# Three chained networks on one core: local attention heads in units of 32 queries and 64 keys, and one block's strided products queued in an earlier group

## The chip, the cores and the metric

The kernel runs on one core of a Trainium2 chip. The metric is the device time of one execution in microseconds, so less is better. Engines are named as in the profile: PE is TensorE (PEld its weight loads), DVE is VectorE, ACT is ScalarE, POOL is GpSimd, and SP is the queue that issues most of the transfers.

## What is computed

An attention over 4 sequences of 576 tokens with 8 heads of 64 is followed by two networks over the 2304 tokens, each fed with the output of the one before. Cut to what matters:

```python
scores = scale * np.matmul(q, k.transpose(0, 1, 3, 2))
rel = pos[:, None] - pos[None, :]
mask_local = (rel >= 0) & (rel < 32)                      # heads 0 to 3
mask_strided = (rel >= 0) & (pos[None, :] % 32 == pos[:, None] % 32)   # heads 4 to 7
attn = softmax(np.where(mask, scores, -1e9))
x = (attn @ v) as 2304 x 512
h = x @ w_in;  x = (h - np.tanh(h)) @ w_out               # d_ff 2048
xn = x / rms(x) * rms_g
x = (silu(xn @ w_gate) * (xn @ w_val)) @ w_out2           # d_ff 1536
```

A query of a local head sees itself and the 31 tokens ahead of it. A query of a strided head sees the tokens of its own residue modulo 32.

## The kernel before, in words

**Blocks and groups.** The tokens are cut into 9 blocks of 256 (block 4 is made of the last 64 tokens of each of the four sequences). The first network runs over five groups of blocks, (0,1), (2,3), (4), (5,6) and (7,8), with 16 steps in each. In a step TensorE makes a tile of h (`ps_h`, 12 matrix products), ACT its tanh, DVE the difference (`tg`, function `dve_g`), ACT and DVE split that in two parts (`g`), and TensorE adds the tile of an earlier step to the output (`ps_x`, 12 products). After the last group the second network follows; it has no attention work in it.

**Attention beside it.** While group g runs, the attention of the blocks of group g+1 is made. Class `Local` has the local heads of a block, and runs in stages: `st_s` (scores, TensorE), `st_m` and `st_e` (mask, maximum, exponential, for each of two halves of 128 queries), `st_n` (normalisation on DVE), `st_p` (transposes on TensorE, into `ps_p`) with `st_c` (copy into `pT`), `st_v` (product with the values, TensorE, into `ps_v`) and `st_o` (copy and split into `xs`, the input of the network). In words of the hand-written opening these are the letters s, m, e, n, p, c, v, y and z. Before the change a unit is 64 queries against 96 keys. The strided heads are either `Dense` (the same stages, with a mask, blocks 0 to 3 and 6) or `Strided` (blocks 4, 5, 7 and 8): there GpSimd multiplies queries by keys (`qk_item`, tile `pr`) and DVE reduces that into `sc`; after a softmax (`soft`, tile `se`) GpSimd multiplies the values by the weights (`pv_item`, tile `pr`), DVE reduces that into `so`, transposes it and splits it into `xs` (`fin`). There are three buffers for `pr`, and one each for the strided queries `sq`, keys `sk` and values `sv`, which `Dense` uses too: a load of them waits until the block before is through with its own.

**What sets the order.** The opening, `START`, is written by hand for all engines. Group 0 is ordered by the compiler's scheduler. From group 1 to group 3 TensorE's order is that of the program; DVE, ACT and GpSimd are ordered by the scheduler, and the SP queue by the scheduler until the last group (in group 0 by hand). `Work` holds two lists for the blocks to come: `.pe`, stages that run at the steps in `STINT`, and `.st`, the strided products, spread over the steps by their size. `EARLY = (5,)` names the block whose strided queries and keys are multiplied in group 1, right behind those of block 4. The products of queries and keys of block 7 stand in the list of group 3 (the fourth), in which the attention of blocks 7 and 8 is made.

```python
SOON = {2: 6, 3: 2}
STINT = {1: (4, 6, 8, 11, 14), 2: (1, 3, 6, 7, 9, 10, 13), 3: (1, 4, 6, 8, 11, 13)}
```

A step runs in this order: h, tanh, the stages of `.pe`, `dve_g`, the items of `.st`, the two parts of g, and then the output product of an earlier step.

Of the kernel before, what the change touches and what calls it, by code (L numbers as in the profile page):

```python
# [33 lines left out]
def attn_moe_moe_kernel(  # L34
# [3 lines left out]
    near_v: bass.AP,  # L38
# [4 lines left out]
    v_loc: bass.AP,  # L43
# [20 lines left out]
    W = 32  # L64
# [34 lines left out]
    EARLY = (5,)  # L99
# [18 lines left out]
    tab = one.tile([128, 544], F32, name="tab")  # L118
    ident, mask, dmask = tab[:, 192:320], tab[:, 320:416], tab[:, 416:544]
    add = tab[:, 0:192].bitcast(BF16)  # L120
    ident16, add = add[:, 0:128], {96: add[:, 128:320].rearrange("q (u t) -> q u t", u=2), 64: add[:, 320:384]}
# [228 lines left out]
    class Heads:  # L350
        def __init__(self, j):
            self.j, self.near, self.early = j, j < NEAR, j < EA
            self.ps, self.sm, self.nm, self.ss, self.pp, self.pT, self.v = {}, {}, {}, {}, {}, {}, {}
            self.slot, self.both, self.sums = {}, None, None
            self.fused = False
# [9 lines left out]
        size = {"sm": 512, "pT": 512, "v": 512}  # L365

        def st_s(self, bank):
# [3 lines left out]
            for hh in range(2):  # L371
                if self.early:
                    m = add[w]
                    m = m.unsqueeze(2) if w == 96 else m.unsqueeze(1).unsqueeze(1)
# [12 lines left out]
        def st_m(self, i):  # L387
# [10 lines left out]
            self.ss[i] = att.tile([128, 2, 2], F32, tag="ss", name="ss", bufs=4)  # L398
            m = dmask if w == 128 else mask if not self.near else add[96][:, i] if w == 96 else add[64]
# [22 lines left out]
        def st_n(self, i):  # L422
            sm, ss = self.sm[i], self.ss.pop(i)
# [3 lines left out]
                out=sm, in0=sm, in1=ss.unsqueeze(3).to_broadcast([128, 2, 2, self.w]), op=ALU.mult  # L427
# [27 lines left out]
    class Local(Heads):  # L455
        w = 96

        def __init__(self, j):
            super().__init__(j)
            self.runs = runs(j)  # L460
            self.at, self.kw = [], 0
            if self.near:
                self.at, self.kw = [0, 32, 96, 160], SUB
            else:
                for _, _, n, _ in self.runs:
                    self.at += range(self.kw, self.kw + n, 64)
                    self.kw += W + n

        def load_qk(self):
# [6 lines left out]
            for b, t0, n, x0 in self.runs:  # L476
# [4 lines left out]
                o = self.at[x0 // 64]  # L481
                nc.sync.dma_start(out=self.kT[:, :, o:o + W + n], in_=k_loc[b, :, :, t0 - W:t0 + n])

        def load_v(self, i):
            if self.early:
                t = held.tile([128, 1024], F32, tag="v", name="v")[0:96]
                nc.sync.dma_start(out=t, in_=near_v[self.j])
                for i in range(2):
                    self.v[i] = t[:, 512 * i:512 * i + 512].rearrange("k (u f) -> k u f", u=2)
                return  # L490
            t = self.room("v", i, 512)[0:96]
            self.v[i] = t.rearrange("k (u f) -> k u f", u=2)
            if self.near:
                nc.sync.dma_start(out=t, in_=near_v[self.j, :, 512 * i:512 * i + 512])
                return
# [943 lines left out]
```

## Time and profile before

| what | value |
|---|---|
| median of 3 runs | 889.43 us (888.55 to 890.35) |
| the profiled execution, its own time | 887.7 us |
| its span | 885.9 us |
| granted clock of TensorE | 0.996 |
| PE busy | 868.8 us (98%) |
| DVE busy | 668.5 us (75%) |
| ACT busy | 397.9 us (45%) |
| POOL busy | 280.0 us (32%) |

The span begins with the first instruction and ends with the last; 1.8 us of the profiled execution's own time lie outside it. The profiled execution is 1.7 us below the median. Times in the rows of the trace count from the start of the span.

### The profile page before, as it was taken

How to read it: one execution, taken by the hardware profiler on the slowest of the kernel's cores; microseconds unless marked ns; L12 is line 12 of the kernel's file. 1: busy time of each engine (PE TensorE's matmuls, PEld its weight loads, DVE VectorE, ACT ScalarE, POOL GpSimd, SP SyncE). 2: the span in 40 equal slices, each digit the busy share in tenths (PEclk: the TensorE clock that was granted, in tenths of full speed). 3: DMA queues.
4: the chain of work that ended last, by engine and by line, in shares of the span. 5: the costliest groups of instructions: out<-in, count | busy, mean ns of one | idle time of the engine just before them, and what ended most of it. 6: DMA issues, size and time to landing. Idle time of an engine off the chain costs nothing.

```text
span 885.9 us, 14105 instructions
## 1 busy us (share of the span) xinstructions
PE 868.8 (98%) x5091; PEld 739.7 (83%) x5091; DVE 668.5 (75%) x1376; ACT 397.9 (45%) x897; POOL 280.0 (32%) x315
## 2 busy tenths in 40 slices
PE   6999999999999999999999999999999999999998
PEld 4888888888998887888887888888878988888986
DVE  5999788888779887179978898576997953445444
ACT  6987643332544333265637553355332533422320
POOL 0000147695276952000000569676442400000000
PEclk8999999999999999999999999999999999999999
DMA  9955224311313000199828777799659139955002
GB/s 328 379 196 173 77 73 151 111 50 36 116 54 110 28 16 1 46 291 346 280 72 270 279 250 270 252 415 364 232 179 349 48 114 355 397 168 166 1 0 84
DMA packets 58566, 157.84 MB, mean 178 GB/s; under 512 B 9536, under 2 KB 20672, under 8 KB 58496
## 3 DMA queue, kind: packets, MB, share of 16 engines
q1 hardware_dynamic: 57344, 155.89, 50.0%
q10 hardware_dynamic: 1152, 1.05, 0.3%
q8 instruction: 40, 0.66, 0.3%
q14 instruction: 30, 0.25, 0.1%
HBM read 119.16 MB, written 37.75 MB: 177 GB/s over the span
## 4 chain that ended last, share of the span: by engine, by line
PE 82%; DVE 8%; POOL 5%; ACT 2%; issue 1%; DMA 1%; SPq 0%; DVEq 0%; POOLq 0%; ACTq 0%
PE ps_x L147 21%; PE ps_h L147 21%; PE ps_pr L147 18%; PE ps_o L147 12%; POOL pr L629 4%; PE ps_m L147 4%; PE ps_q L147 3%; DVE so L669 3%; DMA raw<-in_w_in_dram 1%; PE ps_s L147 1%; POOL pr L662 1%; PE ps_v L147 1%; ACT sm L416 1%; PE ps_p L437 1%; DVE x L957 0%
## 5 line engine op out<-in xcount | busy, mean ns | idle before, releaser
L147 PE MATMUL ps_h<-xs,w 128*128 128x512 f32 (+1 forms) x984 | 213.4, 365 | 0.7 <-DVE tg L814 0.7
L147 PE MATMUL ps_x<-g,w 128*128 128x512 f32 (+1 forms) x984 | 214.0, 366 | 0.0
L147 PEld LDWEIGHTS ps_h<-xs,w 128*128 128x128 f32 x984 | 169.0, 189 | 30.6 <-DVE tg L814 1.1
L147 PEld LDWEIGHTS ps_x<-g,w 128*128 128x128 f32 x984 | 168.6, 189 | 30.0 <-issue 0.2
L147 PE MATMUL ps_pr<-xt,wt 128*128 128x448 f32 x576 | 123.1, 366 | 2.2 <-DVE s L1040 1.4
L629 POOL TENSOR_TENSOR pr<-sk,sq 128x256 f32<-128x256 f32 (+2 forms) x101 | 82.5, 852 | 131.8 <-DMA sq<-in_q_str_dram 126.4
L147 PE MATMUL ps_o<-wt,p 128*128 128x512 f32 x504 | 120.2, 390 | 0.0
L147 PEld LDWEIGHTS ps_pr<-xt,wt 128*128 128x128 f32 x576 | 107.9, 188 | 13.5 <-DVE s L1040 2.2
L147 PEld LDWEIGHTS ps_o<-wt,p 128*128 128x128 f32 x504 | 94.6, 188 | 18.7
L820 ACT CAST g<-tg 128x512 fp32r<-128x512 f32 (+1 forms) x82 | 46.6, 568 | 108.9 <-DVE tg L814 108.8
L662 POOL TENSOR_TENSOR pr<-sv,se 128x288 f32<-128x288 f32 (+12 forms) x104 | 69.7, 691 | 56.7 <-DVE so L669 19.8
L1050 ACT COPY u<-ps_pr 128x448 f32<-128x448 f32 x72 | 38.2, 533 | 84.8 <-PE ps_pr L147 84.7
L814 DVE SCALAR_TENSOR_TENSOR tg<-ps_h,tg 128x512 f32<-128x512 f32 (+1 forms) x82 | 50.8, 619 | 28.0 <-ACT tg L809 28.0
L669 DVE TENSOR_REDUCE so<-pr 128x16 f32<-128x272 f32 (+11 forms) x104 | 65.0, 653 | 8.7 <-POOL pr L662 8.4
L971 POOL TENSOR_TENSOR tr<-x 128x896 f32<-128x896 f32 x4 | 15.1, 3765 | 171.1 <-DMA raw<-in_w_gate_dram 153.9
L809 ACT ACTIVATE tg<-ps_h 128x512 f32<-128x512 f32 (+1 forms) x82 | 44.2, 539 | 48.1 <-PE ps_h L147 48.1
L1101 DVE SCALAR_TENSOR_TENSOR osum<-ps_o,osum 128x512 f32<-128x512 f32 x70 | 47.9, 687 | 21.6 <-PE ps_o L147 20.9
L825 DVE TENSOR_TENSOR g<-tg,g 128x512 fp32r<-128x512 f32 (+1 forms) x82 | 55.3, 677 | 10.8 <-ACT g L820 10.2
L147 PE MATMUL ps_pr<-xt,wo 128*128 128x448 f32 x288 | 60.8, 366 | 0.2 <-ACT u L1050 0.2
L147 PEld LDWEIGHTS ps_pr<-xt,wo 128*128 128x128 f32 x288 | 54.0, 188 | 5.2 <-ACT u L1050 0.6
L184 ACT CAST w<-ct 128x512 fp32r<-128x512 f32 x68 | 42.1, 619 | 30.3 <-DVE ct L177 28.2
L634 DVE TENSOR_REDUCE sc<-pr 128x4 f32<-128x256 f32 (+2 forms) x101 | 43.8, 437 | 12.1 <-POOL pr L629 11.6
(110 smaller groups left out, 1201.4 us busy)
## 6 DMA issues: line engine op xcount, KB each, us to landing
wt<-w SPq DMA_DIRECT2D x84, 512.0 KB, 5.9
raw<-in_w_out_dram SPq DMA_DIRECT2D x28, 512.0 KB, 6.1
raw<-in_w_gate_dram SPq DMA_DIRECT2D x24, 512.0 KB, 5.9
raw<-in_w_val_dram SPq DMA_DIRECT2D x24, 512.0 KB, 6.8
w<-w SPq DMA_DIRECT2D x24, 512.0 KB, 6.6
w<-wo SPq DMA_DIRECT2D x24, 512.0 KB, 8.2
raw<-in_w_in_dram SPq DMA_DIRECT2D x16, 512.0 KB, 9.9
out_dram<-osum SPq DMA_DIRECT2D x18, 256.0 KB, 2.1
```

What stands on the lines that cost most here:

```text
L147: nc.tensor.matmul(out_, lhsT, rhs, start=start, stop=stop, skip_group_check=True)
L184: nc.scalar.copy(out=self.t[:, 0].rearrange("p c f -> p (c f)"), in_=self.b)
L629: nc.gpsimd.tensor_tensor(out=pr, in0=self.k[:, a:e, :], in1=self.q[:, c - c0:c - c0 + 1, :].to_broadcast([128, e - a, D]), op=ALU.mult,)
L634: pend.append(lambda: nc.vector.tensor_reduce(out=s[:, c - c0, a:e], in_=pr, axis=AX.X, op=ALU.add))
L662: nc.gpsimd.tensor_tensor(out=pr, in0=self.v[:, 0:c + 1, a:e], in1=self.e[:, c - c0, 0:c + 1].unsqueeze(2).to_broadcast([128, c + 1, e - a ...
L669: pend.append(lambda: nc.vector.tensor_reduce(out=o[:, c - g0, a:e], in_=pr.rearrange("l c d -> l d c"), axis=AX.X, op=ALU.add))
L809: nc.scalar.activation(out=t, in_=h_of[g, f, a], func=ACTF.Tanh, scale=WS)
L814: nc.vector.scalar_tensor_tensor(out=t, in0=h_of.pop((g, f, a)), scalar=WS, in1=t, op0=ALU.mult, op1=ALU.subtract)
L820: nc.scalar.copy(out=t[:, 0], in_=t_of[g, f, a])
L825: nc.vector.tensor_tensor(out=t[:, 1], in0=t_of.pop((g, f, a)), in1=t[:, 0].bitcast(F32), op=ALU.subtract)
L1050: nc.scalar.copy(out=u, in_=x[kd])
L1101: nc.vector.scalar_tensor_tensor(out=o, in0=ps, scalar=WS, in1=o, op0=ALU.mult, op1=ALU.add)
```

## The change

A local unit is now 32 queries against 64 keys. `st_s` makes 32 products of 32 by 64 in place of 16 of 64 by 96. A row of scores has 64 words in place of 96, so that the two halves of a block's queries fit side by side: `Local` becomes `fused`, as `Dense` of the first blocks is, with one normalisation in place of two, four transposes of 128 by 128 in place of eight of 128 by 96, and one copy into `pT` in place of two. `st_v` makes 32 products of 64 keys by 32 queries in place of 16 of 96 by 64, and writes into two banks in place of one. The values come from a new array `v_win`, laid out on the host, in one transfer of 512 KB in place of two of 192 KB. The table of masks is 480 words wide in place of 544.

`EARLY` is now (5, 7): the products of queries and keys of block 7 stand in a list of their own, `late`, of the third group (g = 2), and run from its ninth step on (`LATE = 8`). The opening is written anew.

```diff
-W9 s0Lx m0L0 e0L0 m0L1 s0Dx n0L0 e0L1 m0D0 p0L0m1 m0D1 s1Lx A0 e0D0 B0 c0L0a n0L1 p0L1h1 P0 Q0 m1L0 m1L1 e0D1 c0L1a
-v0Lh0 s1Dx n0D1 n0D0 A1 e1L0 p0Dh1 e1L1 y0L1 n1L0 m1D0 m1D1 c0Da n1L1 v0Dm0m1 y0L0 e1D0 y0D1 z0L0 y0D0 z0L1 p1L0h1
-c1L0a B1 z0D0 P1 z0D1 p1L1h1 e1D1 c1L1a Q1 n1D0 n1D1 h0h0 A2 v1Lm1 T0 B2 A3 G0 y1L0 p1Dh1 c1Da y1L1 B3 v1Dh1m0 I0 P2
-J0 y1D1 z1L0 y1D0 h1h0 T1 z1L1 z1D1 z1D0 P3 h2h1 Q2 G1 A4 Q3 T2 B4 I1 G2 J1 I2 J2 X0
+W9 s0Lx s0Dx m0L1 m0L0 e0L1 e0L0 m0D1 m0D0 e0D1 n0L p0Lm0 A0 s1Lx B0 e0D0 s1Dx c0La P0 m1L1 A1 v0Lh0h1 m1L0 e1L1 n0D
+e1L0 p0Dm0 Q0 c0Da A2 m1D1 v0Dm0m1 m1D0 n1L y0L1 y0L0 B2 y0D0 y0D1 e1D0 z0D0 z0D1 e1D1 z0L0 p1Lm1 z0L1 h0h0 c1La B1
+n1D P1 T0 P2 v1Lm0m1 y1L0 Q1 G0 y1L1 Q2 p1Dh1 z1L0 z1L1 I0 c1Da J0 A3 h1h0 v1Dh1m0 B3 T1 y1D1 G1 X0 z1D1 y1D0 z1D0 A4
+P3 B4 Q3 I1 h2h0 J1 T2 G2 I2 J2
...
-    EARLY = (5,)
+    EARLY, AHEAD, LATE = (5, 7), (5,), 8
...
+            n = self.unit
             for i in range(2):
                 for p in range(2):
-                    for k in range(2):
+                    for x in range(0, 128, n):
                         for hh in range(2):
-                            r, u = slice(64 * hh, 64 * hh + 64), 2 * i + k
+                            r, t = slice(64 * hh, 64 * hh + 64), 128 * i + x
+                            a = self.at[t // n]
                             mm(
-                                ps[hh][64 * k:64 * k + 64, i, p, :], self.q[r, u, p, :],
-                                self.kT[r, p, self.at[u]:self.at[u] + w], not self.early, True,
+                                ps[hh][x:x + n, i, p, :], self.q[r, t // 64, p, t % 64:t % 64 + n],
+                                self.kT[r, p, a:a + w], not self.early, True,
                             )
...
         def st_n(self, i):
+            if self.fused:
+                sm = self.both.rearrange("q h p i t -> q (h p i) t")
+                ss = self.sums.rearrange("q h p i -> q (h p i)")
...
     class Local(Heads):
-        w = 96
+        w = 64
...
+            self.fused, self.local, self.unit = True, True, W
...
-            t = self.room("v", i, 512)[0:96]
...
+                t = one.tile([128, 1024], F32, tag="v", name="v")
+            self.v = t.rearrange("k (c f) -> k c f", f=256)
+            nc.sync.dma_start(out=t, in_=v_win[self.j])

         def st_v(self, bank):
-            ps = bank("ps_v").rearrange("r (i p u t) -> r i p u t", i=2, u=2, p=2)
...
+            ps = [bank("ps_v")[:, :256].rearrange("r (p t) -> r p t", p=2) for _ in range(2)]
+            pT = self.pT.pop(0)
+            for c in range(4):
+                for p in range(2):
+                    for hh in range(2):
+                        for i in range(2):
+                            h, r, x = 2 * p + hh, slice(64 * i, 64 * i + 64), W * c
                             mm(
-                                ps[64 * hh:64 * hh + 64, i, p, u, :], v[:, u, 64 * h:64 * h + 64],
-                                pT[:, hh, p, 64 * u:64 * u + 64], True, True,
+                                ps[i][64 * hh:64 * hh + 64, p, x:x + W], self.v[r, c, 64 * h:64 * h + 64],
+                                pT[r, hh, p, x:x + W], True, True,
                             )
...
-                    if j + 1 == EARLY[0]:
-                        for o in (strd[i][0] for i in EARLY):
-                            self.st += o.items().qks
...
+            self.st += [x for j in early for x in strd[j][0].items().qks]
+            self.late = [x for j in late for x in strd[j][0].items().qks]
...
-                wks.append(Work(groups[g + 1], EARLY if g == 1 else ()))
+                wks.append(Work(groups[g + 1], *{1: (AHEAD, EARLY[:1]), 2: ((), (), EARLY[1:])}.get(g, ())))
...
+            if f >= LATE:
+                wk.run(wk.late, max(rem, 1))
```

How the change moves instructions is shown at three places. The first is TensorE's queue at the end of the opening: `ps_h<-xs,w` are the first tiles of h, `ps_v<-pT,v` is the value product of block 1's local heads, `ps_p` a transpose, and `ps_v<-pT,dv` the value product of block 1's strided heads. Before, and then after:

```order
L147 MATMUL ps_h<-xs,w 128x256 x12
L147 MATMUL ps_v<-pT,v 64x64 x16
L437 MATMUL ps_p<-tab,sm 128x128 x4
L147 MATMUL ps_v<-pT,dv 32x64 x32
L147 MATMUL ps_h<-xs,w 128x256 x12
```

```order
L146 MATMUL ps_h<-xs,w 128x256 x12
L146 MATMUL ps_v<-pT,v 64x32 x32
L450 MATMUL ps_p<-tab,sm 128x128 x4
L146 MATMUL ps_h<-xs,w 128x256 x12
L146 MATMUL ps_s<-lq 32x64 x8
L146 MATMUL ps_v<-pT,dv 32x64 x32
```

The second tile of h and the first scores of block 2 (`ps_s<-lq`) now stand ahead of the strided value product.

The second place is the SP queue late in the third group. `sk` and `sq` are the strided keys and queries, first of block 7 and then of block 8; `sv` is the strided values of block 7, and `v` the local values. The brackets hold what the row waits for. Before, and then after:

```order
L604 DMA sk_3258<-in_k_str_dram 128x1024 [waits DMAHW1_49,PE_49]
L605 DMA sq_3257<-in_q_str_dram 128x512 [waits DMAHW2_49]
L499 DMA v_3364<-in_v_loc_dram 96x2x256 [waits DMAHW4_49,DMAHW3_49,PE_49]
L499 DMA v_3366<-in_v_loc_dram 96x2x256 [waits DMAHW5_49,PE_49]
L610 DMA sv_3543<-in_v_str_dram 128x1024 [waits DMAHW6_49,PE_49]
L604 DMA sk_3833<-in_k_str_dram 128x1024 [waits DMAHW1_49,Pool_49]
L605 DMA sq_3832<-in_q_str_dram 128x512 [waits DMAHW7_49,DMAHW2_49]
```

```order
L603 DMA sk_3366<-in_k_str_dram 128x1024 [waits DMAHW4_49,PE_49]
L604 DMA sq_3365<-in_q_str_dram 128x512 [waits DMAHW5_49]
L504 DMA v_3499<-in_v_win_dram 128x1024 [waits DMAHW6_49,DMAHW0_49,PE_49]
L603 DMA sk_3770<-in_k_str_dram 128x1024 [waits DMAHW7_49,DMAHW4_49,Pool_49]
L604 DMA sq_3769<-in_q_str_dram 128x512 [waits DMAHW5_49]
L609 DMA sv_3718<-in_v_str_dram 128x1024 [waits DMAHW1_49,PE_49]
```

The strided values of block 7 now stand behind the keys and queries of block 8, which wait for GpSimd.

The third place is DVE's queue in the fourth group, up to a `tg` of its steps, while block 8's strided values are reduced (`so<-pr`) and its local scores normalised (`ss`, `sm<-sm,ss`). Before, and then after:

```order
L424 TENSOR_SCALAR ss<-ss 128x4
L669 TENSOR_REDUCE so<-pr 128x21 x2
L425 RECIPROCAL ss<-ss 128x4
L424 TENSOR_SCALAR ss<-ss 128x4
L426 TENSOR_TENSOR sm<-sm,ss 128x384
L425 RECIPROCAL ss<-ss 128x4
L688 TENSOR_TENSOR xs<-pr,xs 128x2x64
L669 TENSOR_REDUCE so<-pr 128x21
L426 TENSOR_TENSOR sm<-sm,ss 128x384
L669 TENSOR_REDUCE so<-pr 128x21
L669 TENSOR_REDUCE so<-pr 128x22
L814 SCALAR_TENSOR_TENSOR tg<-ps_h,tg 128x512
```

```order
L437 TENSOR_SCALAR ss<-ss 128x8
L438 RECIPROCAL ss<-ss 128x8
L439 TENSOR_TENSOR sm<-sm,ss 128x512
L668 TENSOR_REDUCE so<-pr 128x22
L676 STREAM_TRANSPOSE pr<-so 128x128
L668 TENSOR_REDUCE so<-pr 128x16 x2
L809 SCALAR_TENSOR_TENSOR tg<-ps_h,tg 128x512
```

From the first value product of block 8 to this `tg` 15 reductions of `so` stand before, and 18 after: one more of 128x22 and two of 128x16, with a transpose between them.

## Rows read from the trace of the kernel before

**Rows 1.** The page's first part: busy time, share of the span, instructions.

```profile
PE 868.8 (98%) x5091; PEld 739.7 (83%) x5091; DVE 668.5 (75%) x1376; ACT 397.9 (45%) x897; POOL 280.0 (32%) x315
```

**Rows 2.** The page's fourth part: the chain that ended last, by engine.

```profile
PE 82%; DVE 8%; POOL 5%; ACT 2%; issue 1%; DMA 1%; SPq 0%; DVEq 0%; POOLq 0%; ACTq 0%
```

**Rows 3.** Timeline of PE, end of the opening: start, duration, instruction, [idle before, releaser].

```profile
28.29 0.86 PE L147 MATMUL ps_v<-pT,dv 64*32 64x64 f32 x64 [0.68 <-ACT pT L442]
```

**Rows 4.** Timeline of ACT in the opening.

```profile
16.93 0.67 ACT L170 ACTIVATE ca<-raw 128x512 f32<-128x512 f32 x1 [0.79 <-DMA raw<-in_w_in_dram]
...
26.46 0.38 ACT L809 ACTIVATE tg<-ps_h 128x256 f32<-128x256 f32 x1
```

**Rows 5.** Timeline of PE: two small stages, each with what follows it.

```profile
77.16 0.86 PE L147 MATMUL ps_v<-pT,dv 64*32 64x64 f32 x64
77.95 1.43 PE L147 MATMUL ps_h<-xs,w 128*128 128x512 f32 x5
...
147.50 0.89 PE L147 MATMUL ps_s<-lq 64*64 64x96 f32 x32
148.32 1.90 PE L147 MATMUL ps_x<-g,w 128*128 128x512 f32 x7
```

**Rows 6.** PE's groups by shape, 62 to 345 us: count, busy us, mean ns, idle.

```profile
L437 PE MATMUL ps_p<-tab,sm 128*96 128x128 f32 x48 | 6.2, 272 | 0.0
L147 PE MATMUL ps_v<-pT,v 96*64 96x64 f32 x160 | 5.8, 225 | 0.0
...
L437 PE MATMUL ps_p<-tab,sm 128*128 128x128 f32 x16 | 2.4, 274 | 0.1
...
L147 PE MATMUL ps_s<-dq 64*64 64x64 f32 x32 | 0.7, 224 | 0.0
```

**Rows 7.** Timeline of PE: two waits in the third and fourth group.

```profile
230.19 0.89 PE L147 MATMUL ps_s<-lq 64*64 64x96 f32 x30 [0.54 <-DVE xs L449]
...
335.45 3.05 PE L147 MATMUL ps_h<-xs,w 128*128 128x512 f32 x12 [0.72 <-DVE tg L814]
```

**Rows 8.** Timeline of DVE: the instructions that ended these waits.

```profile
229.64 0.40 DVE L449 TENSOR_TENSOR xs<-ps_v,xs 128x256 fp32r<-128x256 f32 x1
...
334.71 0.68 DVE L814 SCALAR_TENSOR_TENSOR tg<-ps_h,tg 128x512 f32<-128x512 f32 x1
```

**Rows 9.** Timeline of the SP queue, third group.

```profile
244.76 0.33 SPq L604 DMA_DIRECT2D sk<-in_k_str_dram  x1
...
265.68 0.35 SPq L610 DMA_DIRECT2D sv<-in_v_str_dram  x1
267.83 0.35 SPq L604 DMA_DIRECT2D sk<-in_k_str_dram  x1
```

**Rows 10.** DMA issues, 266 to 275 us: count, KB each, us to landing.

```profile
sv<-in_v_str_dram SPq DMA_DIRECT2D x1, 512.0 KB, 3.8
sk<-in_k_str_dram SPq DMA_DIRECT2D x1, 512.0 KB, 3.7
```

**Rows 11.** Timeline of POOL: block 7's strided products.

```profile
249.07 18.73 POOL L629 TENSOR_TENSOR pr<-sk,sq 128x256 f32<-128x256 f32 x23 [20.22 <-DMA sq<-in_q_str_dram]
271.43 2.86 POOL L662 TENSOR_TENSOR pr<-sv,se 128x288 f32<-128x288 f32 x4 [3.63 <-DVE se L652]
```

**Rows 12.** DVE's groups by shape, whole run.

```profile
L426 DVE TENSOR_TENSOR sm<-sm,ss 128x384 f32<-128x384 f32 x18 | 10.8, 598 | 0.2
...
L669 DVE TENSOR_REDUCE so<-pr 128x16 f32<-128x240 f32 x12 | 6.7, 572 | 0.0
...
L677 DVE STREAM_TRANSPOSE pr<-so 128x128 f32<-128x128 f32 x16 | 5.0, 310 | 0.3
...
L425 DVE RECIPROCAL ss<-ss 128x4 f32<-128x4 f32 x28 | 4.7, 172 | 0.5
...
L669 DVE TENSOR_REDUCE so<-pr 128x22 f32<-128x308 f32 x3 | 2.3, 768 | 0.8 <-POOL pr L662 0.8
...
L426 DVE TENSOR_TENSOR sm<-sm,ss 128x512 f32<-128x512 f32 x2 | 1.5, 746 | 0.0
```

More of the change, by code (lines that the diff above doesn't have):

```diff
@@ L397, in st_m @@
             self.nm[i] = nm = att.tile([128, 2, 2], F32, tag="nm", name="nm", bufs=4)
-            self.ss[i] = att.tile([128, 2, 2], F32, tag="ss", name="ss", bufs=4)
-            m = dmask if w == 128 else mask if not self.near else add[96][:, i] if w == 96 else add[64]
+            if not self.fused:
+                self.ss[i] = att.tile([128, 2, 2], F32, tag="ss", name="ss", bufs=4)
+            else:
+                if self.sums is None:
+                    self.sums = att.tile([128, 2, 2, 2], F32, tag="ss", name="ss", bufs=4)
+                self.ss[i] = self.sums[:, :, :, i]
+            if self.local:
+                m = add_l[:, i] if self.near else mask
+            else:
+                m = add_d if self.near else dmask
             for hh in range(2):
@@ L426, in st_n @@
             nc.vector.tensor_tensor(
-                out=sm, in0=sm, in1=ss.unsqueeze(3).to_broadcast([128, 2, 2, self.w]), op=ALU.mult
+                out=sm, in0=sm, in1=ss.unsqueeze(2).to_broadcast(list(sm.shape)), op=ALU.mult
             )
@@ L462, in __init__ @@
             if self.near:
[L463 removed]
+                self.at, self.kw = [max(0, t - W) for t in range(0, SUB, W)], SUB
             else:
                 for _, _, n, _ in self.runs:
[L466 removed]
+                    self.at += range(self.kw, self.kw + n, W)
                     self.kw += W + n
@@ L480, in load_qk, with load_v @@
                 )
-                o = self.at[x0 // 64]
+                o = self.at[x0 // W]
                 nc.sync.dma_start(out=self.kT[:, :, o:o + W + n], in_=k_loc[b, :, :, t0 - W:t0 + n])
-        def load_v(self, i):
+        def load_v(self):
             if self.early:
[L486 to L490, printed above, removed]
-            t = self.room("v", i, 512)[0:96]
[L492 to L495, printed above, removed]
-            at = [b * S + t - W for b, t in subs[self.j][2 * i:2 * i + 2]]
-            first = v_loc[0, 0:96, :]
-            (sp, _), (sf, nf) = first.ap
-            nc.sync.dma_start(
-                out=self.v[i],
-                in_=bass.AP(
-                    tensor=first.tensor, offset=v_loc.offset + at[0] * sp,
-                    ap=[[sp, 96], [(at[1] - at[0]) * sp, 2], [sf, nf]],
-                ),
-            )
@@ L518, in st_v @@
                             )
-            self.po = {i: ps[:, i] for i in range(2)}
+            self.po = {i: ps[i].rearrange("r p (u t) -> r p u t", t=64) for i in range(2)}
         def dst(self, i):
@@ L722, in attn_moe_moe_kernel, with __init__ @@
     class Work:
-        def __init__(self, js, early=()):
+        def __init__(self, js, ahead=(), early=(), late=()):
             self.pe, self.st = [], []
@@ L751, in stage @@
                     o.st_e(i)
-                for i in range(2):
+                for i in range(1 if o.fused else 2):
                     o.st_n(i)
@@ L765, in stage @@
                     nxt.load_qk()
-                if nm == "v" and isinstance(o, Local):
-                    for i in range(2):
-                        nxt.load_v(i)
-                elif nm == "v":
+                if nm == "v":
                     nxt.load_v()
@@ L1227, in attn_moe_moe_kernel @@
                 order.close()
-            assert not wks[-1].pe and not wks[-1].st
+            assert not wks[-1].pe and not wks[-1].st and not wks[-1].late
             new_x(g + 1)
             if g + 1 < NG:
-                wks.append(Work(groups[g + 1], EARLY if g == 1 else ()))
+                wks.append(Work(groups[g + 1], *{1: (AHEAD, EARLY[:1]), 2: ((), (), EARLY[1:])}.get(g, ())))
         if g == NG - 1 and f == 0:
@@ L1403, in lay_out, with windows @@
     v_l = v[:, :4].transpose(0, 2, 1, 3).reshape(B, S, 4 * D)
+    subs = [[(b, t + 64 * u) for u in range(4)] for t in (0, 256) for b in range(B)]
+    subs[B:B] = [[(b, 512) for b in range(B)]]
+    def windows(sub):
+        r = [v_l[b, max(0, t + x - 32):][:64] for b, t in sub for x in (0, 32)]
+        return _np.stack(r).reshape(2, 4, 64, 4 * D).transpose(0, 2, 1, 3).reshape(128, 1024)
     q_d = residues(q, 16).reshape(B, 2, 2, 2, 8, 4, 8, D).transpose(0, 3, 2, 7, 5, 1, 6, 4).reshape(B, 2, 128, 512)
```

54 lines of the change are left out of this document (23 added, 31 removed).

## The prediction

> **What bounds the kernel now.** I read the page's first part for the engines, then its chain of waits, then TensorE's timeline for every wait, and then the timelines of the engines that end those waits. TensorE is busy 98% of the span [rows 1] and holds 82% of the chain that ended last; DVE has 8% of it and GpSimd 5% [rows 2]. So almost everything that leaves TensorE's queue is time, unless the network's steps then wait for DVE or GpSimd. TensorE's timeline shows few waits: the last of the opening ends at 28.29 us, after 0.68 us, on ACT's copy into `pT` [rows 3]. From there on TensorE is fed but for two waits that the change touches. At 230.19 the scores of block 6 wait 0.54 us for `xs`, since one of their banks still holds the value product of block 5. At 335.45 a tile of h waits 0.72 us for `tg` [rows 7], which DVE makes only at 334.71, behind its reductions of strided products [rows 8]. Behind 345 us the network's products follow each other, and the change alters nothing.
>
> Between these two waits lies a second chain, which TensorE starts and which comes back to it. The strided keys of block 7 are loaded at 244.76 [rows 9], right behind TensorE's last use of the same buffer; GpSimd has waited 20.22 us for them, works from 249.07 to 267.80 on block 7's 23 products, waits 3.63 us for the softmax on DVE, and goes on at 271.43 [rows 11]. It and DVE are then busy with blocks 7 and 8 up to the wait at 335.45.
>
> **The change part by part.** The sum is made against the profiled execution's own 887.7 us; its span is 885.9 us, and the median of the runs, 889.43, stands 1.7 us above it.
>
> *1, the opening.* The second tile of h now stands ahead of the value product that waits at 28.29 [rows 3], so that TensorE gets its first continuous work from the first `tg`, which hangs on the tanh at 26.46 [rows 4], and no longer on that copy. ACT has less to do ahead of it (two copies go, and some exponentials are narrower), but its decodes of weights already wait for the DMA, 0.79 us at 16.93 [rows 4], and the opening loads 0.1 MB more. I take the tanh 0.5 us earlier and the feed of TensorE at about 27.2: −1.1 us. Bounds: −2.0 if ACT's whole relief arrives, +0.5 if the loads eat it.
>
> *2, TensorE's work.* A stage is priced from its start to the start of what follows. Scores before: 148.32 − 147.50 = 0.82 us. After they have 64 records of the shape that the strided value product of block 1 has (64*32, 64x64), and that took 77.95 − 77.16 = 0.79 us [rows 5]: −0.03. Transposes: 48 records in six blocks, 6.2 us, so 1.03 us each; after they are four of 128*128, of which 16 took 2.4 us in four stages, 0.60 each [rows 6]: −0.43. Value product: 160 records in five blocks, 5.8 us, less some 0.07 us of overlap each with the next (its group ends later than the next begins), 1.09; after it has 64 records of 64 by 64 against 32 columns. No row has that shape. From below it is bounded by the 0.79 us for 64 records [rows 5]; from above by 64 records at the price of the 64*64 product with 64 columns, 0.7 us for 32 [rows 6], so 1.4. It has half those columns, which brings it to the lower end: I take 0.79, −0.30. A block thus saves 0.76 us. Ahead of the wait for block 7's keys at 244.76 lie blocks 2 to 5 whole and block 6's scores and transposes: 4 x 0.76 + 0.46 = −3.5 us.
>
> A rule speaks against this. The Trainium skill, "TensorE: Matmul & The Clock Gate", section "Wait — 56ns, not 53.3ns?", says that starts of matmuls never come closer than about 25 ns, however few columns they have; "TensorEngine Tiling (Array Packing)", section "Instruction Overhead", warns against dividing a dimension that is small already. By an estimate from that figure, 64 records would take 1.6 us and the change would cost time. The trace disagrees: the strided row has 64 records in 0.79 us, 12.3 ns each [rows 5]. It is a rival below, with terms from rows.
>
> *3, the wait at 230.19.* `st_v` now fills two banks, and block 6's scores need both. On DVE the second half's `xs` stands one reduction later than before, 0.57 us [rows 12], and TensorE comes 0.3 us sooner. The wait grows from 0.54 [rows 7] to about 1.3: +0.8. Bounds: −0.5 (it vanishes) and +1.0.
>
> Elsewhere the second bank costs nothing: other small stages stand one step or more apart, which is over 5 us of h and output products, and an evacuation is 0.40 us [rows 8].
>
> *4, the chain from 244.76 to 335.45.* Putting block 7's products in the third group's ninth step moves nothing on GpSimd: they already run there, because their load waits for TensorE at 244.76 [rows 9, 11]. What moves is SP's queue. Before, the strided values of block 7 were issued at 265.68, ahead of block 8's keys, and took 3.8 us, so they were there at 269.5, before GpSimd wanted them at 271.43. Now they stand behind block 8's keys and queries, which wait for GpSimd's last product of block 7, so they go at 267.83 or later [rows 9], as the last 512 KB of 1.28 MB. One 512 KB load takes 3.7 us [rows 10]; three in a row, partly overlapped, I put at 5.1 us, landing at 272.9: +1.5 (bounds 0 and +3). Then DVE: one normalisation in place of two saves 2 x 0.60 − 0.75 us of multiplication and two small operations of 0.17 [rows 12], −0.8, for block 7 and again for block 8. Last, three more reductions stand ahead of the `tg` that TensorE waits for, 0.77 + 2 x 0.57, and a transpose of 0.31 [rows 12]: +2.2. Together 1.5 − 0.8 − 0.8 + 2.2 = +2.1. TensorE's savings inside this stretch, some 1.1 us, only lengthen its wait at `tg`, from 0.72 to about 3.9 us in all.
>
> *5, behind 335.45.* Block 8's transposes and value product: −0.43 − 0.30 = −0.7.
>
> The wider value load (0.1 MB more) is hidden by the steps between load and use; the shorter table of masks only helps the opening. Exponentials and masks keep or lose width and lie beside TensorE's work.
>
> Sum: −1.1 − 3.5 + 0.8 + 2.1 − 0.7 = −2.4; 887.7 − 2.4 = 885.3, and as a median **887.0 us**. Its own range is 885.5 to 888.5.
>
> **The rivals.** *A, the second chain doesn't bind:* the values land in time and the extra reductions find room, as GpSimd's 3.63 us of idle ahead of 271.43 allows [rows 11]. Then all seven blocks count, 7 x 0.76 = 5.3 (blocks 2 to 8), with terms 1 and 3: −1.1 − 5.3 + 0.8 − 0.7 (the old wait goes) = −6.3, a median of 883.1. Against it: the wait at 335.45 exists already, so every delay on that chain is paid.
>
> *B, the value product at its upper price:* 1.4 us, +0.31 in place of −0.30, makes term 2 −0.6 − 0.46 = −1.1 and term 5 −0.1; with 1, 3 and 4 the sum is +0.6, 890.0. If only the opening gives nothing, it is −1.3, 888.1. Between them lies no measurable change.
>
> *C, slower: records have a floor.* Scores before had 32 records in 0.82 us, 25.6 ns each [rows 5]. If TensorE can't go faster per record, both 64-record stages take 1.64: scores +0.82, value product +0.55, transposes −0.43. Term 2 becomes 4 x 0.94 + 0.39 = +4.2, term 5 +0.1, the sum −1.1 + 4.2 + 0.8 + 2.1 + 0.1 = +6.1, 895.5. With P for 64 records, the sum is 10 P − 10.3 us, so it is slower by over 0.2% (1.8 us) from P = 1.21 on, 19 ns a record. For it: the 32 records of 64*64 [rows 6]. Against it: the 12.3 ns of the strided row [rows 5], whose shape the scores take over exactly. The rule of the Trainium skill named above ends here.
>
> *D, the late queue does nothing:* this is in the forecast already, as far as GpSimd's order goes.
>
> **How the numbers follow.** Chances: the forecast 0.50, A 0.25, B 0.15, C or a load of the values that lands another 4 us later 0.10. The likeliest gives the time, 887.0. The range reaches from a little below A, 882.3, to B's upper end, 890.2, and leaves out C and the far side of A. A measurement of this kernel tells 0.2% (1.8 us, so 887.65 and 891.2) from no change: of the forecast's 0.50 I put 0.36 on faster and 0.14 on the same, A is faster, B the same: faster 0.61, same 0.29, slower 0.10.
>
> **What would show it.** Right: the profile of the changed kernel has scores and value products of 64 records in about 0.8 us to the next start, transposes x4 in 0.4 to 0.6; TensorE fed from about 27.2; a wait of about 1.3 us of `ps_s` on `xs` near 226; GpSimd's first value product of block 7 released by the DMA of `sv`; and 3 to 4 us of waiting for `tg` some 90 us behind block 7's key load. Wrong: no wait for `tg` there (A), a value product of over 1.2 us (B or C), or a GpSimd that starts block 7's products much earlier or later against TensorE than 4.3 us behind the load.

## The result, and the profile after

The changed kernel takes 894.41 us (median of 12 runs) beside 890.23 us for the kernel before, measured together: a ratio of 1.0059, 95% interval 1.0041 to 1.0076, so it is slower by about 5 us (the medians are 4.2 us apart). The forecast was 887.0 us, in a range of 882.3 to 890.2. The profiled execution took 893.45 us (5.75 more than the one of before), with a span of 891.6.

The first and the fourth part of the page of the kernel after, which answer to [rows 1, 2]:

```profile
PE 869.0 (97%) x5631; PEld 738.6 (83%) x5631; DVE 663.4 (74%) x1337; ACT 391.1 (44%) x888; POOL 281.4 (32%) x315
...
PE 55%; DVE 12%; POOL 5%; DMA 3%; issue 2%; ACT 0%; SPq 0%; DVEq 0%; POOLq 0%; ACTq 0%
```

DVE and ACT have shed work as the change says, and TensorE has not: 869.0 us where 868.8 stood. The chain after is followed back only to 190 us, so that its shares add up to 77% of the span, and PE's 55% can't be set beside the 82% of before; DVE holds 12% where it had 8, and the DMA 3% where it had 1. Where the time went is read from the starts of a few stages that both kernels have on TensorE:

| stage on TensorE | before, us | after, us | shift | forecast |
|---|---|---|---|---|
| scores of block 4 (second group) | 147.50 | 147.60 | +0.1 | −2.6 |
| strided scores of block 6 (third group) | 243.57 | 242.84 | −0.7 | −3.8 |
| scores of block 8 (fourth group) | 319.97 | 318.93 | −1.0 | −4.9 |
| transposes of block 8 | 338.34 | 343.13 | +4.8 | −1.7 |
| value product of block 8 | 350.22 | 354.57 | +4.4 | −2.1 |
| end of the span | 885.9 | 891.6 | +5.7 | −2.4 |

Two things stand out: the gain of the first 150 us is missing, and between block 8's scores and transposes nearly 6 us are lost. Of the second, TensorE's timeline before, from which the stretch of 18.37 us is read, and after, with the waits that answer to the second of [rows 7]:

```profile
319.97 0.89 PE L147 MATMUL ps_s<-lq 64*64 64x96 f32 x32
...
338.34 1.04 PE L437 MATMUL ps_p<-tab,sm 128*96 128x128 f32 x8
```

```profile
318.93 0.86 PE L146 MATMUL ps_s<-lq 64*32 64x64 f32 x64
...
330.20 3.03 PE L146 MATMUL ps_h<-xs,w 128*128 128x512 f32 x12 [1.61 <-DVE tg L809]
333.06 2.88 PE L146 MATMUL ps_x<-g,w 128*128 128x512 f32 x12
338.68 4.61 PE L146 MATMUL ps_h<-xs,w 128*128 128x512 f32 x12 [2.73 <-DVE tg L809]
343.13 0.60 PE L450 MATMUL ps_p<-tab,sm 128*128 128x128 f32 x4
```

Waits of 1.61 and 2.73 us for `tg`, 4.3 in all where 0.72 stood; and then a tile of h that takes 4.61 us, not 3.05. The windows of the stretch 338.7 to 342.7 give its granted clock as 0.59 of full speed (the columns are the stretch, the busy time of PE, PEld, DVE, ACT and POOL, the clock, DMA share and GB/s):

```profile
338.70:342.70 4.00, 4.00 (x11) 3.13 (x12) 4.00 (x8) 0.58 (x1) 2.94 (x5) 0.59 0.00 2
```

TensorE ran at 1.2 GHz, the lower of its two levels, for most of that tile: 3.6 us of additional waiting and 1.6 us of slow clock make 5.2 of the 5.8 us lost there; the rest lies in small pieces. GpSimd's timeline after answers to [rows 11]:

```profile
248.09 18.55 POOL L628 TENSOR_TENSOR pr<-sk,sq 128x256 f32<-128x256 f32 x23 [19.89 <-DMA sq<-in_q_str_dram]
272.32 2.67 POOL L661 TENSOR_TENSOR pr<-sv,se 128x288 f32<-128x288 f32 x4 [5.68 <-DMA sv<-in_v_str_dram]
...
318.39 2.67 POOL L661 TENSOR_TENSOR pr<-sv,se 128x288 f32<-128x288 f32 x4 [3.69 <-issue]
```

Block 7's value products are now released by the DMA of `sv`, 28.3 us behind the key load (issued at 244.03), where they came 26.7 behind it. The `tg` of the long wait follows block 8's first value product on GpSimd, at 318.39, by 19.6 us, where it was 17.3:

```profile
337.94 0.68 DVE L809 SCALAR_TENSOR_TENSOR tg<-ps_h,tg 128x512 f32<-128x512 f32 x1
```

### The profile page after: what moved, and what is told of

It is laid out like the page before. It is cut to its first block, busy times and chain, and to the rows that moved or that the text cites. A ratio compares the mean times of both kernels' runs of the same rounds, so it can differ in the third digit from the quotient of the medians.

```text
span 891.6 us, 15109 instructions
## 1 busy us (share of the span) xinstructions
PE 869.0 (97%) x5631; PEld 738.6 (83%) x5631; DVE 663.4 (74%) x1337; ACT 391.1 (44%) x888; POOL 281.4 (32%) x315
## 4 chain that ended last, share of the span: by engine, by line
PE 55%; DVE 12%; POOL 5%; DMA 3%; issue 2%; ACT 0%; SPq 0%; DVEq 0%; POOLq 0%; ACTq 0%
PE ps_pr L146 18%; PE ps_o L146 12%; PE ps_x L146 10%; PE ps_h L146 10%; DVE so L668 4%; POOL pr L628 4%; PE ps_q L146 3%; PE ps_m L146 2%; DMA raw<-in_w_val_dram 1%; DVE wa L276 1%; DVE wa L277 1%; DVE g L820 1%; POOL pr L661 1%; POOL tr L966 1%; DMA raw<-in_w_gate_dram 1%
## 5 line engine op out<-in xcount | busy, mean ns | idle before, releaser
L146 PE MATMUL ps_h<-xs,w 128*128 128x512 f32 (+1 forms) x984 | 216.1, 368 | 4.8 <-DVE tg L809 4.7
L146 PEld LDWEIGHTS ps_h<-xs,w 128*128 128x128 f32 x984 | 171.5, 192 | 36.2 <-DVE tg L809 6.6
```

The costliest lines, as they stand in the source:

```text
L146: nc.tensor.matmul(out_, lhsT, rhs, start=start, stop=stop, skip_group_check=True)
```

## The experiments

Two theories stood against each other for the fourth group. **DVE's order:** the scheduler put more of block 8's reductions ahead of the `tg` that TensorE waits for, counted from block 8's softmax: 3, 9 and 15 reductions ahead of the first three `tg` before the change, 4, 11 and 18 after. **GpSimd's chain:** the values of block 7 land late, and all that follows is late with them. For the missing gain of the first 150 us the suspects were the price of the new value product, the order that the scheduler gave to group 0, and the opening.

### tg_first_11 and tg_first_10: DVE by the program for one and for two steps

```diff
+        if g == 3 and f == 11:        # tg_first_10: f == 10
+            dvq = ctx.enter_context(ExitStack())
+            dvq.enter_context(tc.manual_schedule(engines={mybir.EngineType.DVE}))
         unit(g, f, a, e, pe_work, work)
+        if g == 3 and f == 11:
+            dvq.close()
```

> The changed kernel with DVE in the order of the program in the 12th step (f = 11) of the fourth group: the tg that TensorE waits longest for (2.7 us, at 338.7) then stands behind 13 of block 8's reductions, not 18; GpSimd's, SP's and TensorE's order there stay as they are. Theory (DVE's order decides that wait, and the clock falls because of it): the 2.7 us wait is gone, the wait of 1.6 us at 330 stays, the h tile takes about 3.0 us and not 4.6, so some 4.3 us less than the changed kernel, about as long as the kernel before (ratio 0.999 to 1.003). Rival (GpSimd's chain, late by the values' landing, decides): the tg moves, but TensorE waits as long a step later, for g or for the next tg.

> The same with DVE in the order of the program in the 11th and the 12th step: the two tg that TensorE waits for then stand behind 8 reductions, not 11 and 18. Theory: both waits, 4.3 us in all, and the stretch at the lower clock, 1.6 us, are gone; 5.9 us less than the changed kernel, 0 to 2 us less than the kernel before (ratio 0.997 to 1.001). Rival: block 8's reductions are late by then and the waits come back at g or at the first tile of the last group.

With one step, the ratio to before is 1.0032 (1.0006 to 1.0057); from block 8's scores to its transposes it is 20.44 us, 3.76 less than the changed kernel's 24.20 (4.3 was expected). The wait of 2.73 us and the slow tile are gone, the one of 1.61 stays, and one of 0.78 is new. With two steps, the ratio is 0.9976 (0.9954 to 0.9999), and the stretch is 18.31 us (before: 18.37). TensorE's timeline of the kernel with two steps:

```profile
324.63 3.04 PE L146 MATMUL ps_h<-xs,w 128*128 128x512 f32 x12 [0.75 <-DVE tg L809]
...
330.22 2.88 PE L146 MATMUL ps_h<-xs,w 128*128 128x512 f32 x12
...
335.66 2.88 PE L146 MATMUL ps_h<-xs,w 128*128 128x512 f32 x12
338.38 0.60 PE L450 MATMUL ps_p<-tab,sm 128*128 128x128 f32 x4
```

The same two tiles that waited now start at once and take 2.72 us to the next start; a wait of 0.75 us is left, about as long as the one before the change. GpSimd pays for it, with an idle time of 7.6 us in the middle of block 8's products, and nothing follows from that: GpSimd is through at 348.2, and TensorE has no wait between 345 and 400 us:

```profile
336.40 1.30 POOL L661 TENSOR_TENSOR pr<-sv,se 128x273 f32<-128x273 f32 x2 [7.63 <-DVE so L668]
...
344.19 4.05 POOL L661 TENSOR_TENSOR pr<-sv,se 128x240 f32<-128x240 f32 x6 [0.41 <-DVE xs L687]
```

So another order of DVE takes away the whole loss of the fourth group, and the late values by themselves don't make it: here GpSimd began block 7's value products 29.1 us behind the key load, later than in the changed kernel. Measured a second time, beside another kernel:

> The kernel with two tg put first once more, beside the one with joined stages on the same chip. Theory: 0.1 to 0.4% faster than the kernel before, 0.1 to 0.2% slower than the joined one. Rival (the first measurement was luck): within 0.1% of before.

The ratio is 0.9986 (0.9956 to 1.0016); it wasn't slower than joined, which has 1.000. Both measurements point to a kernel some 1 to 2 us faster than the one before; the second interval takes in no change, and no more is claimed. Why the scheduler put more reductions ahead of `tg` isn't shown.

### sp_by_program: block 7's values ahead of block 8's keys

```diff
+            if g == 2:
+                queue2 = ctx.enter_context(ExitStack())
+                queue2.enter_context(tc.manual_schedule(engines={mybir.EngineType.SP}))
             if g == NG - 1:
+                queue2.close()
                 order.close()
```

> The changed kernel with the SP queue in the order of the program from the third group on: block 7's strided values are then loaded ahead of block 8's keys and queries. Theory (their late landing is 1.6 us of the 4.3 us that TensorE waits for tg): GpSimd's first value product of block 7 is released by DVE's softmax and comes about 26.7 us behind the key load, not 28.3; TensorE waits 2.5 to 3 us for tg in all, and the kernel is 1.6 us faster than the changed one, 3 us if the clock then stays up. Rival (DVE's order alone sets tg): the landing moves and the waits for tg stay at 4 to 4.5 us.

The ratio is 1.0057 (1.0031 to 1.0083), so nothing is gained, and from block 8's scores to its transposes it is 24.03 us, where the changed kernel has 24.20. GpSimd's and TensorE's timelines:

```profile
271.57 4.40 POOL L661 TENSOR_TENSOR pr<-sv,se 128x288 f32<-128x288 f32 x6 [3.77 <-DVE se L651]
...
318.18 2.67 POOL L661 TENSOR_TENSOR pr<-sv,se 128x288 f32<-128x288 f32 x4 [3.42 <-issue]
```

```profile
331.82 3.02 PE L146 MATMUL ps_h<-xs,w 128*128 128x512 f32 x12 [1.35 <-DVE tg L809]
340.18 4.61 PE L146 MATMUL ps_h<-xs,w 128*128 128x512 f32 x12 [2.62 <-DVE tg L809]
```

The landing is mended: DVE's softmax releases the products again, 26.3 us behind the key load at 245.23. The waits stay, as the rival said: the scheduler answered the earlier values with yet another order of DVE, with 7, 14 and 22 reductions ahead of the first three `tg`. TensorE also waits 1.66 us for `tg` in the second group, where it waits 0.39 in the changed kernel. So this run doesn't test the landing by itself: 14 and 22 reductions ahead of the two `tg` cost 3.97 us of waiting here, 11 and 18 cost 4.34 in the changed kernel, so that an earlier landing under an unchanged order of DVE may be worth something. That isn't measured.

### filled_wait: work for TensorE in the long wait

```diff
+        if g == 3 and f == 11:
+            ps = bank_m("ps_w")
+            for n in range(12):
+                mm(ps, w1["in", f].t[:, 0, n % 4, :], xs[g][:, 0, n % 4, :], n == 0, n == 11)
         pe_h(g, f, a, e)
```

> The changed kernel with 12 products of 128x512 put on TensorE ahead of the h tile of the fourth group's 12th step, which waits 2.7 us for tg in the changed kernel and then takes 4.6 us where 3.05 is usual. Theory (the wait lets TensorE's clock fall): the tile takes about 3.0 us, the granted clock stays at full speed there, and the kernel is about 1.5 us faster than the changed one (888.5 to 893.5 us beside a before of 888 to 890). Rival (the clock falls for another reason, or the tile is slow for its operands): the tile still takes over 4 us and the time is that of the changed kernel.

The ratio is 1.0021 (1.0000 to 1.0043). The added products fill the wait, and the tile behind them takes 3.02 us:

```profile
338.43 2.88 PE L146 MATMUL ps_w<-xs,w 128*128 128x512 f32 x12
341.37 3.02 PE L146 MATMUL ps_h<-xs,w 128*128 128x512 f32 x12
344.23 0.60 PE L450 MATMUL ps_p<-tab,sm 128*128 128x128 f32 x4
```

The granted clock of 338.7 to 342.7 is 1.00: without the wait the clock doesn't fall there. From block 8's scores to its transposes it is 23.34 us, 0.86 less than in the changed kernel: 1.6 us of clock won, and 0.76 of a new wait for `tg` at 325. The gain by the two ratios, 3.4 us, is larger than this stretch explains; about 1 us more stands behind a wait of 0.87 us in the second network that this execution hadn't, and the rest is inside the two intervals.

### v_halves and v_by_bank: what the value product costs

```diff
# v_halves
+                            for y in (0, 32):
                                 mm(
-                                    ps[i][64 * hh:64 * hh + 64, p, x:x + W], self.v[r, c, 64 * h:64 * h + 64],
+                                    ps[i][64 * hh + y:64 * hh + y + 32, p, x:x + W],
+                                    self.v[r, c, 64 * h + y:64 * h + y + 32],
                                     pT[r, hh, p, x:x + W], True, True,
# v_by_bank
-            for c in range(4):
-                for p in range(2):
-                    for hh in range(2):
-                        for i in range(2):
+            for i in range(2):
+                for c in range(4):
+                    for p in range(2):
+                        for hh in range(2):
```

> The changed kernel with each value product of a local unit made in two halves of 32 of the 64 dimensions: 128 records of 64*32 with 32 columns in place of 64 of 64*64 with 32 columns. The value product took 1.07 us to the next start in the changed kernel, where 0.79 had been predicted. Theory (a record costs what loading its 64 columns of weights takes, and not what streaming 32 columns takes): a half costs half, so the stage takes 1.0 to 1.1 us again. Rival (a floor for each record, near the 10 to 12 ns of the 64*32 rows): 1.3 to 1.6 us.

> The changed kernel with the value product of a local unit issued bank by bank: first all 32 products of the lower 64 rows, then all of the upper 64 rows, where they alternate in the changed kernel. In group 0 the changed kernel has block 3's value product in this order (16 and 16 in two pieces, 1.06 us for a half of 32 records). Theory (two products on different rows run side by side only if they alternate; this order, not the cuts alone, is what group 0 lost): the 64 records of a stage in the second group take 1.9 to 2.1 us to the next start, not 1.07, and each stretch with one is 0.8 to 1.0 us longer. Rival (the order within a stage is free): 1.07 us.

Each of these two kernels, and split_stages below, ran once, for its profile. Their whole times (904.23, 896.08 and 897.21 us) hold whatever clock the opening had, and aren't compared; stages are. A record is one matrix instruction of the trace, which has two for each of these products.

TensorE's timeline of the second group: block 4's value product and what follows it, first in the changed kernel, then in v_halves, then in v_by_bank:

```profile
170.90 1.14 PE L146 MATMUL ps_v<-pT,v 64*64 64x32 f32 x64
171.96 3.02 PE L146 MATMUL ps_x<-g,w 128*128 128x512 f32 x12
```

```profile
178.58 1.29 PE L146 MATMUL ps_v<-pT,v 64*32 64x32 f32 x128
179.80 1.42 PE L146 MATMUL ps_x<-g,w 128*128 128x512 f32 x5
```

```profile
174.19 1.85 PE L146 MATMUL ps_v<-pT,v 64*64 64x32 f32 x64
175.97 2.34 PE L146 MATMUL ps_x<-g,w 128*128 128x512 f32 x9
```

From start to start: 1.06 us for 64 records, 1.22 for 128 of half the width, 1.78 for the 64 issued bank by bank. Half the width costs 9.5 ns a record, the whole 16.6, so neither theory holds to the letter: most of the price goes with the columns of weights, and some with each record. The number of columns that stream counts for little: block 3's strided scores, 64*64 with 64 columns, took 0.62 us for 32 records before the change (19 ns each, with the switch to the next tile spread over half as many records). And the alternation is worth 0.72 us of 1.78. That was forecast at 0.8 to 1.0; the direction holds, the size is a little less. The loop that v_by_bank moves outward picks the half of the rows and the bank together, so no run shows which of the two must alternate.

This matters in group 0, where the scheduler orders TensorE. There the changed kernel has block 3's value product in two halves, each on one half of the rows and one bank, the first behind strided scores that also come half by half:

```profile
97.40 0.51 PE L146 MATMUL ps_s<-dq 64*64 64x64 f32 x10
...
97.89 0.93 PE L146 MATMUL ps_v<-pT,v 64*64 64x32 f32 x26
98.75 3.03 PE L146 MATMUL ps_x<-g,w 128*128 128x512 f32 x12
...
102.16 1.12 PE L146 MATMUL ps_v<-pT,v 64*64 64x32 f32 x32
103.22 0.97 PE L146 MATMUL ps_h<-xs,w 128*128 128x512 f32 x3
```

The 26 and the 32 records take 0.86 and 1.06 us, 33 ns each. From starts of single records, the value products of blocks 2 and 3 take 3.07 us in group 0 (2.16 before) and the strided scores 2.62 (1.85 before).

### split_stages: what a cut costs

Three stages of the second group (scores and value product of block 4, scores of block 5) are issued in four pieces, each followed by three of the 12 output products of that step; nothing else is added.

> The changed kernel with three small stages of the second group (scores and value product of block 4, scores of block 5) cut in four pieces each, with three output products of 512 columns between the pieces: 9 more cuts, no other work. Theory (a cut costs about 0.25 us on TensorE, and group 0's cuts are what the changed kernel lost there): the stretch from block 4's scores to block 6's scores is 2.0 to 2.5 us longer than the changed kernel's 81.6 us. Rival (a cut costs nothing): it is the same within 0.3 us.

```profile
148.86 0.34 PE L146 MATMUL ps_s<-lq 64*32 64x64 f32 x16
149.13 0.96 PE L146 MATMUL ps_x<-g,w 128*128 128x512 f32 x3
150.02 0.34 PE L146 MATMUL ps_s<-lq 64*32 64x64 f32 x16
```

From block 4's scores to block 6's it is 83.69 us, where the changed kernel has 81.56: 2.13 us for 9 cuts, or 2.5, since the changed kernel has a wait of 0.39 us there that this one hasn't. A cut costs 0.24 to 0.28 us.

### joined and whole_stages: mending group 0

In joined, the score stages and value products of group 0 are each issued in the order in which they are written (DVE as in tg_first_10); in whole_stages TensorE follows the program in group 0 altogether.

> The kernel with two tg put first (DVE in the order of the program in the 11th and 12th step of the fourth group), and in group 0 each stage of scores and each value product in the order in which it is written, so that its products alternate between two banks. Theory (group 0 lost 1.5 to 1.8 us by its order): block 4's scores start 1.0 to 1.8 us earlier behind the first tile of 512 columns than in the changed kernel (110.7 us), and it is 1 to 2 us faster than the kernel with two tg put first (ratio to before 0.995 to 0.998). Rival: the stretch stays at 110.7 us, and so does the time.

> The changed kernel with TensorE in the order of the program in group 0 too: every small stage of blocks 2 and 3 stands in one piece (one of scores was in 5 pieces, several others in 2 to 4). Theory (each cut costs about 0.25 us in going to small products and back): the start of block 4's scores comes 1.5 to 1.8 us earlier than 147.6 us, if no stage waits; the kernel is 0.5 to 2 us faster than the changed one. Rival (cuts cost nothing, the loss in group 0 is elsewhere): block 4's scores start at 147.6 or later.

Neither gained. In joined the small stages of group 0 cost 8.4 us rather than 9.5, as expected, but block 4's scores start 110.45 us behind the first tile of 512 columns, and 110.68 in the changed kernel: 0.27 us came back as a wait for a part of the weights, and 0.6 us more lies in the large tiles, unexplained. The theory's 1.0 to 1.8 us at this place isn't there; the rival came true. The ratio is 1.000 (0.9973 to 1.0027), with a wait of 1.62 us for `tg` in the second group, which the order of DVE there brings. In whole_stages TensorE waits for what the scheduler had covered, 7.1 us in the first 150, where the changed kernel waits for nothing behind its opening, and block 4's scores start at 158.28; the ratio is 1.0164 (1.0139 to 1.0188), and its timeline has

```profile
38.99 4.61 PE L146 MATMUL ps_h<-xs,w 128*128 128x512 f32 x12 [2.81 <-DVE tg L809]
...
93.83 1.08 PE L450 MATMUL ps_p<-tab,sm 128*128 128x128 f32 x4 [3.00 <-DVE sm L439]
```

In these two runs the cuts of group 0 were traded for waits and slower large tiles. That 1.5 us or more could be won there isn't shown.

### old_opening: the new local heads with the old order of the opening

The words of the opening before are kept in their order, with n, p and c of the two halves as one word each, and the value product on two banks.

> The changed kernel with the opening in the order of before (the words for the two halves' normalisations, transposes and copies taken together, the value product on two banks). Theory (the new opening gains 0.85 us at the first tile of 512 columns, the rest of the loss lies behind it): the first 12 products of 512 columns start with the work ahead of them done about 0.5 to 1 us later, and the kernel is 0 to 2 us slower than the changed one, by how group 0 is cut up. Rival (the new opening with its longer stretch at the lower clock costs the time): it is 1 us or more faster than the changed one.

The ratio is 1.0069 (1.0050 to 1.0088), 0.1% above the changed kernel's and within its interval. In its profile block 4's scores start at 152.72 us, 5 us later; but its TensorE had a granted clock of 0.74 over the first 40 us, and 0.87 in the changed kernel's profile, so that the order and the clock can't be told apart. What the opening alone is worth stays open.

## Why the prediction was wrong, step by step

By the table, the 8.1 us between the forecast of −2.4 and the profile's +5.7 lie in four places: 2.7 up to block 4's scores, 1.2 from there to block 8's scores, 2.6 from these to block 8's transposes, and 1.6 behind. The steps that failed are 2 (the price of the value product, and the order of group 0 at nothing), 4 (the length of the second chain and what it does to TensorE) and the clock, which had no term.

**Step 1, the opening, came out right in size, and in part by luck.** The first tile of 512 columns starts at 36.92 us, 2.2 later than before, but with 24 more products of 256 columns (2.87 us from the starts of single records) and the rest of block 2's scores (0.47 us) done: 1.1 us ahead, as forecast. But TensorE is fed without a wait from 21.59 on, where about 27.2 was forecast, and the first tile of h then takes 2.84 us to the next start where it took 1.60, at a granted clock of 0.50:

```profile
21.59 1.12 PE L450 MATMUL ps_p<-tab,sm 128*128 128x128 f32 x4 [1.79 <-DVE xs L462]
22.36 2.91 PE L146 MATMUL ps_h<-xs,w 128*128 128x256 f32 x12
...
36.92 2.91 PE L146 MATMUL ps_h<-xs,w 128*128 128x512 f32 x12
```

So more relief arrived than was counted on, and the lower clock took some of it back. In other kernels with this opening the first tile of 512 columns starts between 36.75 (sp_by_program) and 39.28 us (filled_wait), so that one profile can't confirm a gain of 1.1. The larger value load was also misread: the opening has two, of 0.13 MB more each.

**Step 2 failed in two terms.** The scores were right (148.42 − 147.60 = 0.82 us with the switch, 0.79 in group 0) and so were the transposes (0.35 us, 0.44 saved). The value product was put at the lower bound, 0.79 us, because it has half the columns of the row at the upper bound; it takes 1.06. The columns that stream were the wrong quantity: the bound to take was the row of the same weights, 64*64, not the row of the same count. That costs 0.27 us for each of five blocks, 1.4 us. And the order of group 0 was priced at nothing: there the loss is the difference between what the stages should cost, 1.1 + 0.9 us ahead of before at block 4's scores, and what is there, 0.1 behind: 2.1 us. By their prices, the strided scores and value products that stand in halves on one bank make 1.7 of it; but joined, which took 1.1 of that away, won only 0.2 us at block 4's scores, so that this isn't shown to be what a better order would give back. The halves stood in TensorE's order, as two rows of 16 products of block 3; the prediction compared orders only where a wait was known. From the first tile of 512 columns to block 4's scores the profiles with this order in group 0 agree within 0.12 us, so the opening's clock has no part in this loss.

**Step 3 failed to the good side.** The wait of block 6's scores is 0.48 us, not 1.3: the value product came no earlier, and DVE's `xs` not later.

**Step 4 had the mechanism and missed its size and its consequence.** The landing was forecast at +1.5 us and is +1.6. The three more reductions and the transpose were forecast at +2.2, and the `tg` is 2.2 us later behind GpSimd's first value product of block 8. But the 0.8 us twice that the fused normalisation saves on DVE was booked as a gain of this chain, and it isn't there: from GpSimd's first value product of block 7 to that of block 8 it is 46.1 us after and 46.0 before. The chain is 3.9 us longer, not 2.1. The landing, a term of the forecast, doesn't make the loss alone: with the late landing and two `tg` first the loss is gone (tg_first_10), and with the landing mended it stayed, though under a longer row of reductions (sp_by_program). In the runs with the late landing the waits go with the number of reductions that DVE has ahead of the two `tg`: 4.3 us with 11 and 18, none with 8 and 8. What an early landing would be worth at 11 and 18 isn't shown. TensorE's waits were forecast at 3.9 us and are 4.3, which is near for the wrong reason: the chain is 1.8 us longer than forecast, and TensorE saved 0.3 us in that stretch, not 1.1.

**The clock was in no step.** Waits on TensorE were booked at their length. Here the tile behind the second of two ran at the lower level and cost 1.6 us more; with the wait filled, it didn't (filled_wait).

**Step 5:** transposes −0.44, value product nothing. From block 8's value product to the end the changed kernel is 1.4 us longer, which the forecast hadn't: waits of 3.9 us behind 345 us rather than 3.0 make 0.9 of it, in instructions whose order on TensorE the change doesn't alter. The one wait that is new, 0.87 us, is 0.34 to 0.95 us in seven other profiles with the same second network and absent in filled_wait and before; its cause stays open.

**Rival D, that the late queue does nothing, holds exactly.** The changed kernel written with `EARLY = (5,)` has the same instructions in the same order on all five engines. Rival A's premise, that the chain doesn't bind, was wrong as the kernel stands. Rival C was wrong: the scores have 64 records in 0.79 us, 12 ns each, and the rule of the Trainium skill ("TensorE: Matmul & The Clock Gate", "Wait — 56ns, not 53.3ns?") of about 25 ns from start to start doesn't describe them. B's price, 1.4 us, was too high, and its direction was right.

## What to carry to other kernels

Where a scheduler orders the engines, a change of a stage's shape can move that order far from the stage, and the move can cost more than the stage saves: compare the whole order of the saturated engine and of the one that it waits for, not only the places with a known wait. Price a small matrix product by the row with weights of the same shape, and ask whether neighbours in the queue alternate between rows and banks. A saving on an engine that isn't the bound of its stretch is no term of the sum, and a wait of the bounding engine that is forecast at several us needs a second term, for a clock that may fall behind it.

## What the runs showed of the hardware that was not expected

- 64 records that alternate between the halves of the rows, and with them between two banks, take 1.06 us; the same 64, first all of one half and then all of the other, take 1.78 us.
- Leaving tiles of 512 columns for a small stage and coming back costs 0.24 to 0.28 us.
- TensorE's clock fell behind some waits and not behind others of the same length: behind 1.61 and 2.73 us in the changed kernel (the tile behind took 4.61 us) and behind 0.38 and 2.87 in v_halves, but not behind 0.93 and 2.73 in v_by_bank. What decides isn't shown. First v_halves, then v_by_bank:

```profile
345.72 4.62 PE L146 MATMUL ps_h<-xs,w 128*128 128x512 f32 x12 [2.87 <-DVE tg L811]
```

```profile
342.84 3.02 PE L146 MATMUL ps_h<-xs,w 128*128 128x512 f32 x12 [2.73 <-DVE tg L809]
```

- In the opening the clock differs from one profile to the next, also for the same kernel: over the first 40 us it was granted at 0.83 in tg_first_10 and at 0.79 in its second measurement, beside 0.91 before and 0.87 after. The end of the opening moves with it by up to 2.5 us, and a single profile of an opening shows little.
- Four of the profiles have a wait of 2.4 us in the second network, between 541 and 560 us, that the others lack. In tg_first_10, whose profiled execution is the slowest of its twelve (892.92 us), and in v_halves the tile behind it ran at the lower clock; in tg_first_again and whole_stages it didn't. The first of these:

```profile
541.72 4.61 PE L146 MATMUL ps_m<-xn,w 128*128 128x512 f32 x12 [2.41 <-DVE s L885]
```
